# ScalarE and VectorE in source order in an attention loop, GpSimd too at a layer's end, weights split one sum sooner

## The chip, the cores and the metric

The kernel runs on one core of a Trainium2 chip. The metric is the device time of one execution in microseconds. The engines are named as in the profile: PE (TensorE, matmuls), PEld (its weight loads), ACT (ScalarE), DVE (VectorE), POOL (GpSimd) and SP (SyncE, which issues the DMAs here).

## The reference

Two layers, each an attention and a spectral filter on x of 2048 rows by 1024 columns, in float32:

```python
def attn(x, wqkv, wo):                 # 32 heads of 32 columns
    q, k, v = split_heads(x @ wqkv)
    p = softmax(q @ k.T * 32 ** -0.5)
    return merge_heads(p @ v) @ wo
def spec(x, w_r, w_i):
    return irfft2(rfft2(x) * (w_r + 1j * w_i))
for _ in range(2):
    x = x + attn(layernorm(x), wqkv, wo)
    x = x + spec(layernorm(x), w_r, w_i)
```

## The kernel before

**The attention's tiles.** The 32 heads are worked on in 8 groups of four, g = 0 to 7. For one group the 2048 queries are taken in 4 chunks c of 512, and the keys in 16 tiles kt of 128. One (g, c, kt) is called a unit here. A unit has three parts. `S` makes the scores with 12 matmuls (L540) into two PSUM tiles `s`, and ACT takes the exp of each (L544, 128x1024) into a tile `p`. `PV` multiplies them with V (16 matmuls, L550). `add` sums the two `p` tiles into two accumulators on DVE (L561 for the first pair of units of a chunk, L563 for the others). The pool of `p` tiles has eight buffers, four units' worth.

**A chunk's end.** `fin` sums the accumulators over the keys with 8 matmuls (L569, called z in this document), and DVE turns, inverts and turns back the sums and scales the chunk's output with them (L570 to L576). `out` splits it into two f16 halves `ohl`: ACT casts the high one (L582), POOL subtracts for the low one (L583).

**Filler.** All products but PV use f16 high and low halves. While group g runs through its 64 units, PE also makes the q, k and v sums of later groups, a few matmuls behind every second unit: `qk_chunk` (24 matmuls a sum, L327) and `v_tiles` (L371). A q or k sum ends in `split`: ACT writes the high half from PSUM (L166) and DVE the low one (L167); POOL squares it (L331) for a bound on the scores (L344, L346). A v sum needs ACT alone. There is one PSUM bank for these sums (`psX`), so the next sum's first matmul waits until its split is done.

**Weights.** `Weights.prep` is a generator for the weights of one phase (the k, q or v sums of one group). It asks for its first three pieces by DMA (L247), then with each step splits one piece (L166, L167; in layer 0 also a maximum, L256 and L257). A q or k weight has two pieces, a v weight four (`wv`). `filler` steps the preparation of the next phase once after each sum.

**The last two groups.** In g=6 `load_wo` splits the projection's weights, and `wo_parts` starts the output projection over the groups that are done (L429, 42 matmuls a tile of 128 rows, drained by DVE at L449). In g=7 `wo_rest` adds the last group's share to 12 of the 16 row tiles: 6 matmuls, then DVE adds (L458), takes statistics (L460, L481), and the tile is written out.

**A layer's end.** The last four row tiles need the last chunk. `first` does their matmuls over the other groups, `last` the rest, with statistics. Every tile is layer-normed for the spectral stage, which wants it folded: `fold` adds and subtracts two halves on POOL (L145, L146), and the fold is scaled on DVE (L160, L161). The scale is a power -0.5 on POOL (L120) and one Newton step on DVE (L121 to L124). `fold_rests` does the 12 earlier tiles with one power for all. The spectral stage starts with transposes on PE (L742), whose every first operand takes rows from all 16 tiles.

**What sets the order.** The loop stands in a manual schedule for PE alone: PE does its instructions in the order of the source. On ACT, DVE, POOL and SP a scheduler places them at build time. In the source, `add` follows `S` by two units: in the step of unit u the scores of u come first, then PV and the adds of u-2, then a piece of filler.

Of the kernel before, what the change touches and what calls it, by code (L numbers as in the profile page):

```python
# [6 lines left out]
F32 = mybir.dt.float32  # L7
# [5 lines left out]
ALU = mybir.AluOpType  # L13
# [99 lines left out]
    return st  # L113


def ln_scale(nc, sm, cst, mv, n=1):

    v, r, q = (sm.tile([128, n], F32, name=f"{c}{n}") for c in "vrn")
    nc.vector.tensor_scalar(v, mv[:, 1::2], 1e-5, None, op0=ALU.add)
    nc.gpsimd.tensor_tensor(r, v, cst["mhalf"].broadcast_to([128, n]), op=ALU.pow)  # L120
    nc.vector.tensor_mul(q, r, r)  # L121
    nc.vector.tensor_mul(q, q, v)
    nc.vector.tensor_scalar(q, q, -0.5, 1.5, op0=ALU.mult, op1=ALU.add)
    nc.vector.tensor_mul(r, r, q)  # L124
    return r


def ln_stats(nc, sm, cst, st, mv):

    nc.vector.bn_aggr(mv, st)  # L130
    return ln_scale(nc, sm, cst, mv)


def layernorm(nc, sm, cst, x, out):
# [6 lines left out]
def fold(nc, x, out, a):  # L141

    xv = x.rearrange("p (a u g q) -> p g a u q", a=8, g=2, q=8)[:, :, a]
    ov = out.rearrange("p (u g a q) -> p g a u q", g=2, a=8, q=8)[:, :, a]
    nc.gpsimd.tensor_tensor(ov[:, 0], xv[:, 0], xv[:, 1], op=ALU.add)  # L145
    nc.gpsimd.tensor_tensor(ov[:, 1], xv[:, 0], xv[:, 1], op=ALU.subtract)  # L146


def fold_norm(nc, sm, cst, st, out):

    mv = sm.tile([128, 2], F32, name="mv")
    r = ln_stats(nc, sm, cst, st, mv)
    b = sm.tile([128, 1], F32, name="b")
    nc.vector.tensor_scalar(b, mv[:, 0:1], 2.0, None, op0=ALU.mult)
    norm_folded(nc, out, out, b, r)


def norm_folded(nc, x, out, b, r):
    xv, ov = (a.rearrange("p (u g q) -> p g u q", g=2, q=64) for a in (x, out))
    nc.vector.tensor_scalar(ov[:, 0], xv[:, 0], b, r, op0=ALU.subtract, op1=ALU.mult)  # L160
    nc.vector.tensor_scalar(ov[:, 1], xv[:, 1], r, None, op0=ALU.mult)  # L161
# [8 lines left out]
def run(g):  # L170
    for _ in g:
        pass
# [93 lines left out]
def attention(nc, tc, layer, ap, xin, yd, wts, wo, cst, dram, flags):  # L266
# [6 lines left out]
    sq, on, on2, sm = ap.sq, ap.on, ap.on2, ap.sm  # L273
# [109 lines left out]
    def sums(ph):  # L383
        return 8 if ph[0] == "v" else 4

    def filler():
        run(prep(phases[0]))
        for i, ph in enumerate(phases):
            nxt = prep(phases[i + 1]) if i + 1 < len(phases) else iter(())
            for n in range(sums(ph)):  # L390
                yield from (v_tiles if ph[0] == "v" else qk_chunk)(ph, n)
                next(nxt, None)
            run(nxt)


# [27 lines left out]
    def wo_mm(p, c, t, n, ds, start=True, stop=True):  # L423

        for d in ds:
            oh, ol = ((olast[c][:, i] if d == 7 else osb[c][:, i, d])[:, t * 128:t * 128 + 128] for i in range(2))
            wh, wl = (wo_t[i][d // 4][:, d % 4, n * 512:n * 512 + 512] for i in range(2))
            for i, (a, b) in enumerate(((oh, wh), (oh, wl), (ol, wh))):
                nc.tensor.matmul(p, a, b, start=start and d == ds[0] and i == 0, stop=stop and d == ds[-1] and i == 2)  # L429
                yield  # L430
# [21 lines left out]
    def wo_last(c, t, p, src, y, start):  # L452

        for n in range(2):
            run(wo_mm(p[:, n], c, t, n, (7,), start=start))
        st = sm.tile([128, 2, 6], F32, name="st")
        r0 = c * 512 + t * 128
        nc.vector.scalar_tensor_tensor(y, p.rearrange("p n c -> p (n c)"), 1.0 / (SO * SW), src, op0=ALU.mult, op1=ALU.add)  # L458
        for n in range(2):
            nc.vector.bn_stats(st[:, n], y[:, n * 512:n * 512 + 512])  # L460
        nc.sync.dma_start(yd[r0:r0 + 128, :], y)
        return st
# [14 lines left out]
    mvs = sm.tile([128, 24], F32, name="mvs")  # L477
# [4 lines left out]

    def fold_rests():

        r = ln_scale(nc, sm, cst, mvs, 12)
        b = sm.tile([128, 12], F32, name="b12")
        nc.vector.tensor_scalar(b, mvs[:, 0::2], 2.0, None, op0=ALU.mult)
        for t in SPILL + [t for t in range(12) if t not in SPILL]:
            o = ap.x[:, t]
            f = o if t in SPILL else pp.tile([128, 1024], F32, name="xn", tag="p")  # L490
            fold(nc, wo_dst[t], f, slice(0, 8))
            norm_folded(nc, f, o, b[:, t:t + 1], r[:, t:t + 1])


# [16 lines left out]
    for c in range(NCH):  # L511
        t = 4 * c + 4
# [44 lines left out]
    def add(g, c, kt):  # L557
        for hf in range(2):
            p = P[g, c, kt, hf]
            if kt == 1:  # L560
                nc.vector.scalar_tensor_tensor(acc[hf], P[g, c, 0, hf], 1e-34, p, op0=ALU.add, op1=ALU.add)  # L561
            elif kt:
                nc.vector.tensor_add(acc[hf], acc[hf], p)  # L563
# [25 lines left out]
    pend, done, late = [], [], []  # L589
# [3 lines left out]
    def slots(f, sums, n, steps):  # L593

        while sums:
            k = max(1, int(n / sums + 0.5))
            m = -(-steps // k)
            for i in range(0, steps, m):
                while left_norms:
                    norms()  # L600
                for _ in range(min(m, steps - i)):
                    next(f, None)
                n -= 1
                yield sums - (i + m >= steps)
            sums -= 1

    with tc.manual_schedule(engines={mybir.EngineType.PE}):
        for g in range(NG):
            todo = sum(sums(ph) for ph in beside.get(g, []))
            sl = slots(fill, todo, 22 if g == NG - 2 else 32, 24)  # L610
            wsl = slots(wof, 4, 10, 21)
            for u in range(NCH * NKT):
                c, kt = divmod(u, NKT)
                S(g, c, kt)
                if kt % 2 == 0:
                    for w in pend:
                        PV(*w)
                    late = pend
                    pend = []
                for w in late[:1]:  # L620
                    add(*w)
                    if w[2] == NKT - 1:
                        fin(*w[:2])
                        done = [w[:2]]
                late = late[1:]
                if kt == 5 and done:
                    out(*done.pop())
                pend.append((g, c, kt))
                if kt % 2 == 0:
                    continue  # L630
                if todo:
                    todo = next(sl)
                elif g == NG - 2:
                    if left:
                        run(lwo)
                        left = 0
                    if next(wsl, None) is not None and u == NCH * NKT - 1:
                        run(wsl)
                elif g == NG - 1:
                    t = rests[0] if rests else 16  # L640
                    if (t // 4 < c - 1 or t // 4 == c - 1 and kt >= 7) and (kt % 4 == 3 or not parts):
                        wo_rest(rests.pop(0))
                    elif parts:
                        parts -= 1
                        for _ in range(21):
                            next(wof)
                if g == NG - 2 and todo < 4:
                    for _ in range(2):
                        if left > (8 if todo == 3 else 0):
                            next(lwo, None)  # L650
                            left -= 1
        for w in pend:
            PV(*w)
        for w in late + pend:
            add(*w)
        run(wof)
        for t in rests:
            wo_rest(t)
        ps, xs = [], []

        def first(t, ds):
            if ds[0] == 0:
                ps.append(psS.tile([128, 2, 512], F32, name="s"))
                xs.append(xres(3, t))
            for n in range(2):
                run(wo_mm(ps[t][:, n], 3, t, n, ds, start=ds[0] == 0, stop=False))

        def last(t):
            o = ap.x[:, 12 + t]
            st = wo_last(3, t, ps[t], xs[t], xs[t], False)  # L670
            fold(nc, xs[t], o, slice(0, 8))
            fold_norm(nc, sm, cst, st, o)
        first(0, range(7))
        fin(NG - 1, NCH - 1)
        out(NG - 1, NCH - 1, nc.vector)
        fold_rests()
        first(1, range(7))
        last(0)
        first(2, range(7))
        last(1)  # L680
        first(3, range(4))
        last(2)
        first(3, range(4, 7))
        last(3)
    psum.close()
    small.close()

# [491 lines left out]
```

## Time and profile before

| | us |
|---|---|
| median of 3 runs | 4025.53 (4022.86 to 4028.82) |
| the profiled execution's own time | 4029.87 |
| its span in the trace | 4028.0 |
| ACT's exps, L544, 2048 of them | 2163.9 busy |
| DVE's adds, L563, 1792 of them | 2163.1 busy |
| POOL | 634.9 busy |
| z of the last chunk, layer 0 and 1 | at 1696.31 and 3690.98 |
| first spectral transposes (L742), layer 0 and 1 | at 1758.13 and 3759.27 |

The span is one execution, taken by the profiler; sums of the prediction are made against its own time. A profile line names a source line, an engine, an operation and its tiles (out<-in); a wait stands in brackets as the idle time ahead of an instruction and who ended it. Idle time counts only on the engine that bounds a stage.

### The profile page before, as it was taken

What the parts mean: (1) busy time and instruction counts of PE and PEld (TensorE: products, weight loads), DVE (VectorE), ACT (ScalarE), POOL (GpSimd) and SP (SyncE); (2) the same over time, 40 slices, a digit from 0 to 9 for tenths busy, and PEclk for the clock granted to TensorE, in tenths of its full rate; (3) what the DMA queues carried; (4) which work ended last, traced back from release to release, by engine and by line L of the source; (5) the groups of instructions that cost most, each with busy time, mean ns of one, the idle gap of its engine ahead of it and who ended that gap; (6) DMA issues with size and microseconds to landing.
All of it is one profiled execution on the core that took longest, in us unless ns stands there. A gap on an engine that the chain in (4) does not pass through costs nothing. (4 is left out here: it accounts for less than half of the span.)

```text
span 4028.0 us, 80149 instructions
## 1 busy us (share of the span) xinstructions
PE 3791.8 (94%) x33204; PEld 1680.2 (42%) x33204; DVE 3257.1 (81%) x3897; ACT 2863.0 (71%) x3533; POOL 634.9 (16%) x585
## 2 busy tenths in 40 slices
PE   7999999999999999979989999999999999997898
PEld 5322423342234233368854234233422432332787
DVE  6789888888988977766766898888889889788456
ACT  4677777787778866448746787788878888663485
POOL 1111011101110100314321110111011101003143
PEclk9999999999999999989989999999999999999999
DMA  3000000000000211143120000000000002121333
GB/s 114 19 22 17 7 22 14 14 9 22 17 12 7 87 51 66 53 152 125 57 84 14 27 17 7 22 17 14 7 22 17 12 9 87 53 72 49 141 101 100
DMA packets 97561, 177.32 MB, mean 44 GB/s; under 512 B 7201, under 2 KB 52897, under 8 KB 96161
## 3 DMA queue, kind: packets, MB, share of 16 engines
q1 hardware_dynamic: 97040, 172.03, 12.7%
q8 instruction: 262, 4.29, 0.5%
q14 instruction: 115, 0.93, 0.1%
q10 hardware_dynamic: 144, 0.07, 0.0%
HBM read 123.83 MB, written 48.23 MB: 43 GB/s over the span
## 5 line engine op out<-in xcount | busy, mean ns | idle before, releaser
L544 ACT ACTIVATE p<-s,bias 128x1024 f32<-128x1024 f32 x2048 | 2163.9, 1111 | 534.6 <-PE s L540 527.9
L563 DVE TENSOR_TENSOR R<-R,p 128x1024 f32<-128x1024 f32 x1792 | 2163.1, 1259 | 163.2 <-ACT p L544 160.7
L550 PE MATMUL o<-p,R 128*32 128x512 f32 x8192 | 996.0, 604 | 0.0
L327 PE MATMUL x<-big,wqk 128*128 128x512 f16 x2880 | 678.6, 380 | 18.0 <-DVE R L167 9.3
L540 PEld LDWEIGHTS <-R 32*128 32x128 f16 x12288 | 239.1, 92 | 845.6 <-issue 728.6
L540 PE MATMUL s<-R 32*128 32x512 f16 x6144 | 444.4, 380 | 49.2 <-ACT p L544 44.4
L540 PE MATMUL s<-Q,R 32*128 32x512 f16 x6144 | 442.2, 378 | 27.8 <-ACT p L544 16.7
L327 PEld LDWEIGHTS <-wqk 128*128 128x128 f16 x3072 | 276.8, 98 | 449.1 <-issue 162.8
L550 PEld LDWEIGHTS o<-p,R 128*32 128x32 f32 x8192 | 214.8, 109 | 529.7 <-issue 529.1
L371 PEld LDWEIGHTS <-big 128*128 128x128 f16 x3072 | 291.9, 98 | 102.3 <-issue 56.3
L371 PE MATMUL x<-wv,big 128*128 128x256 f16 x2688 | 321.1, 275 | 5.9 <-DVE big L167 2.9
L561 DVE SCALAR_TENSOR_TENSOR R<-p 128x1024 f32<-128x1024 f32 x128 | 153.9, 1204 | 195.6 <-ACT p L544 195.6
L331 POOL TENSOR_TENSOR sq<-R 128x512 bf16<-128x512 f16 x96 | 149.3, 1555 | 970.8 <-ACT R L166 970.6
L583 POOL TENSOR_TENSOR ohl<-zt,ohl 128x512 f16<-128x512 f32 x62 | 83.2, 1342 | 1178.4 <-ACT ohl L582 1178.4
L429 PE MATMUL x<-big 128*128 128x512 f16 x1008 | 228.0, 380 | 0.0
L429 PEld LDWEIGHTS <-big 128*128 128x128 f16 x1344 | 126.8, 98 | 177.6 <-issue 35.4
L582 ACT CAST ohl<-zt 128x512 f16<-128x512 f32 x64 | 39.6, 618 | 140.0 <-DVE zt L576 98.6
L861 DVE TENSOR_TENSOR H<-G,H 128x512 f16<-128x512 f32 (+1 forms) x68 | 46.7, 687 | 104.1 <-ACT H L860 104.0
L331 POOL TENSOR_TENSOR sq<-Q 128x512 bf16<-128x512 f16 x32 | 48.9, 1529 | 444.6 <-ACT Q L166 444.6
L813 PE MATMUL ps<-cbi,H 128*128 128x256 f16 (+1 forms) x792 | 99.1, 273 | 5.6 <-ACT H L860 3.7
L806 ACT COPY U<-ps 64x256 f32<-64x256 f32 (+1 forms) x272 | 97.0, 357 | 7.8 <-PE ps L813 2.6
L806 ACT COPY B<-ps 64x256 f32<-64x256 f32 (+1 forms) x272 | 97.0, 356 | 6.7 <-PE ps L813 2.4
(417 smaller groups left out, 3256.3 us busy)
## 6 DMA issues: line engine op xcount, KB each, us to landing
wst<-in_wp SPq DMA_DIRECT2D x96, 256.0 KB, 2.8
R<-y SPq DMA_DIRECT2D x32, 512.0 KB, 5.2
w<-in_w SPq DMA_DIRECT2D x60, 256.0 KB, 2.7
od<-ohl SPq DMA_DIRECT2D x56, 256.0 KB, 2.4
big<-od SPq DMA_DIRECT2D x16, 896.0 KB, 6.4
y<-R SPq DMA_DIRECT2D x20, 512.0 KB, 2.6
R<-in_x SPq DMA_DIRECT2D x16, 512.0 KB, 6.8
wst<-in_wo SPq DMA_DIRECT2D x32, 256.0 KB, 3.1
```

The source lines that it names most:

```text
L327: nc.tensor.matmul(ps, a, b, start=d == 0 and i == 0, stop=d == 7 and i == 2)
L331: nc.gpsimd.tensor_tensor(nrm[ph][:, c], t[:, 0], t[:, 0], op=ALU.mult)
L371: nc.tensor.matmul(ps[:, j], l, r, start=d == 0 and i == 0, stop=d == 7 and i == 2)
L429: nc.tensor.matmul(p, a, b, start=start and d == ds[0] and i == 0, stop=stop and d == ds[-1] and i == 2)
L540: nc.tensor.matmul(s[h // 2][:, h % 2], K[g][r, a, kt * 128:kt * 128 + 128], Q[g][r, b, c * 512:c * 512 + 512], start=i == 0, stop=i == 2)
L544: nc.scalar.activation(p, s[hf], AF.Exp, bias=bias[g], scale=SCALE / (SQ * SQ))
L550: nc.tensor.matmul(O[g, c][32 * h:32 * h + 32], V[g][:, kt, 32 * h:32 * h + 32], P[g, c, kt, h // 2][:, h % 2], start=kt == 0, stop=kt == ...
L561: nc.vector.scalar_tensor_tensor(acc[hf], P[g, c, 0, hf], 1e-34, p, op0=ALU.add, op1=ALU.add)
L563: nc.vector.tensor_add(acc[hf], acc[hf], p)
L583: eng.tensor_tensor(t[:, 1], r, t[:, 0], op=ALU.subtract)
L806: nc.scalar.copy(ov[64 * r:64 * r + 64, a0:a0 + m, x], tl[64 * x:64 * x + 64, :m, r])
L813: nc.tensor.matmul(out, l, r, start=k == 0, stop=k == len(mm_) - 1)
```

## The change

1. In the loop ACT and DVE are put under manual order as well: they too do their instructions in the order of the source.
2. After the loop's last projections a second manual schedule begins, for PE, ACT, DVE and POOL.
3. `ln_scale` is parted into `ln_root` (variance, power on POOL) and `ln_newton`. `fold_rests` becomes a generator, stepped fold by fold between the last tiles. `last` does statistics, power and fold of a last tile, a new `scale` its Newton step and norm.
4. At the end of the loop the adds that are left (`late`) come before the last PV, and each PV is followed by its own add.
5. `filler` steps the preparation of the next weights twice after each sum but a phase's first.

```diff
-def ln_scale(nc, sm, cst, mv, n=1):
+def ln_root(nc, sm, cst, mv, n=1):
-    v, r, q = (sm.tile([128, n], F32, name=f"{c}{n}") for c in "vrn")
+    v, r = (sm.tile([128, n], F32, name=f"{c}{n}") for c in "vr")
     nc.vector.tensor_scalar(v, mv[:, 1::2], 1e-5, None, op0=ALU.add)
     nc.gpsimd.tensor_tensor(r, v, cst["mhalf"].broadcast_to([128, n]), op=ALU.pow)
+    return v, r
+def ln_newton(nc, sm, v, r, n=1):
+    q = sm.tile([128, n], F32, name=f"n{n}")
     nc.vector.tensor_mul(q, r, r)
...
                 yield from (v_tiles if ph[0] == "v" else qk_chunk)(ph, n)
-                next(nxt, None)
+                for _ in range(1 + (n > 0)):
+                    next(nxt, None)
...
             fold(nc, wo_dst[t], f, slice(0, 8))
+            yield
             norm_folded(nc, f, o, b[:, t:t + 1], r[:, t:t + 1])
...
-    with tc.manual_schedule(engines={mybir.EngineType.PE}):
+    E = mybir.EngineType
+    with tc.manual_schedule(engines={E.PE, E.Activation, E.DVE}):
...
+        for w in late:
+            add(*w)
         for w in pend:
             PV(*w)
-        for w in late + pend:
             add(*w)
         run(wof)
         for t in rests:
             wo_rest(t)
-        ps, xs = [], []
+    with tc.manual_schedule(engines={E.PE, E.Activation, E.DVE, E.Pool}):
+        ps, xs, sc, folds = [], [], {}, fold_rests()
...
         def last(t):
-            o = ap.x[:, 12 + t]
-            st = wo_last(3, t, ps[t], xs[t], xs[t], False)
-            fold(nc, xs[t], o, slice(0, 8))
-            fold_norm(nc, sm, cst, st, o)
+            st = wo_last(3, t, ps[t], xs[t], xs[t], False)
+            mv = sm.tile([128, 2], F32, name="mv")
+            nc.vector.bn_aggr(mv, st)
+            b = sm.tile([128, 1], F32, name="b")
+            nc.vector.tensor_scalar(b, mv[:, 0:1], 2.0, None, op0=ALU.mult)
+            sc[t] = (b, *ln_root(nc, sm, cst, mv))
+            fold(nc, xs[t], ap.x[:, 12 + t], slice(0, 8))
+
+        def scale(t):
+            b, v, r = sc[t]
+            o = ap.x[:, 12 + t]
+            norm_folded(nc, o, o, b, ln_newton(nc, sm, v, r))
+
+        def some(n):
+            for _ in range(n):
+                next(folds, None)
         first(0, range(7))
         fin(NG - 1, NCH - 1)
         out(NG - 1, NCH - 1, nc.vector)
-        fold_rests()
+        some(8)
         first(1, range(7))
         last(0)
+        some(2)
+        scale(0)
         first(2, range(7))
+        some(2)
         last(1)
+        run(folds)
+        scale(1)
         first(3, range(4))
         last(2)
         first(3, range(4, 7))
+        scale(2)
         last(3)
+        scale(3)
```

PE's order stays as it was but for a few rows. Up to the loop the line numbers of the changed kernel are higher by 5 to 7: its L172 is L167 of before, L568 is L561, L570 is L563, L577 to L583 are L570 to L576, L150 and L151 are L145 and L146, L126 to L129 are L121 to L124.

DVE before, in the last chunk of g=0 in layer 1: adds (into R, from p), the low halves of three k sums (R<-x,R) and of a weight (wqk), and then the next chunk's first add with `fin`'s first step (zt).

```order
L563 TENSOR_TENSOR R<-R,p 128x1024 x8
L167 SCALAR_TENSOR_TENSOR R<-x,R 128x512
L563 TENSOR_TENSOR R<-R,p 128x1024 x12
L167 SCALAR_TENSOR_TENSOR R<-x,R 128x512
L563 TENSOR_TENSOR R<-R,p 128x1024 x8
L167 SCALAR_TENSOR_TENSOR R<-x,R 128x512
L167 SCALAR_TENSOR_TENSOR wqk<-wst,wqk 128x512 x2
L561 SCALAR_TENSOR_TENSOR R<-p 128x1024
L570 STREAM_TRANSPOSE zt<-s 128x512
```

DVE after, in the same chunk, from its first two units' adds to `fin`'s first step.

```order
L568 SCALAR_TENSOR_TENSOR R<-p 128x1024 x2
L570 TENSOR_TENSOR R<-R,p 128x1024 x4
L172 SCALAR_TENSOR_TENSOR R<-x,R 128x512
L570 TENSOR_TENSOR R<-R,p 128x1024 x4
L172 SCALAR_TENSOR_TENSOR wqk<-wst,wqk 128x512 x2
L570 TENSOR_TENSOR R<-R,p 128x1024 x8
L172 SCALAR_TENSOR_TENSOR R<-x,R 128x512
L570 TENSOR_TENSOR R<-R,p 128x1024 x8
L172 SCALAR_TENSOR_TENSOR R<-x,R 128x512
L570 TENSOR_TENSOR R<-R,p 128x1024 x4
L577 STREAM_TRANSPOSE zt<-s 128x512
```

Each low half of a sum stands four adds sooner: the first behind the adds of units 1 to 3 (it stood behind unit 5), the last ahead of the chunk's last four adds (it stood behind them). `fin` no longer has adds of the next chunk between its steps.

POOL before, at the end of layer 0: the last `ohl` of the loop, folds (R or xn) of the 12 earlier tiles, and the power for all twelve (r, from v).

```order
L583 TENSOR_TENSOR ohl<-zt,ohl 128x512 x5
L145 TENSOR_TENSOR R<-R 128x8x8x8
L146 TENSOR_TENSOR R<-R 128x8x8x8
L145 TENSOR_TENSOR R<-wv 128x8x8x8 x2
L146 TENSOR_TENSOR R<-wv 128x8x8x8 x2
L145 TENSOR_TENSOR xn<-R 128x8x8x8
L146 TENSOR_TENSOR xn<-R 128x8x8x8
...
L145 TENSOR_TENSOR xn<-R 128x8x8x8
L120 TENSOR_TENSOR r_18270<-v_18269,mhalf 128x12
L146 TENSOR_TENSOR xn<-R 128x8x8x8
L145 TENSOR_TENSOR xn<-R 128x8x8x8
```

POOL after, at the same place; the power with `128x1` belongs to last tile 0, whose folds read xres.

```order
L590 TENSOR_TENSOR ohl<-zt,ohl 128x512 x5
L120 TENSOR_TENSOR r_18273<-v_18272,mhalf 128x12
L150 TENSOR_TENSOR R<-R 128x8x8x8
L151 TENSOR_TENSOR R<-R 128x8x8x8
L150 TENSOR_TENSOR R<-R 128x8x8x8
L151 TENSOR_TENSOR R<-R 128x8x8x8
...
L150 TENSOR_TENSOR xn<-R 128x8x8x8
L151 TENSOR_TENSOR xn<-R 128x8x8x8
L120 TENSOR_TENSOR r_18378<-v_18377,mhalf 128x1
L150 TENSOR_TENSOR R<-xres 128x8x8x8
L151 TENSOR_TENSOR R<-xres 128x8x8x8
L150 TENSOR_TENSOR xn<-R 128x8x8x8
```

The power for twelve tiles was behind most of the folds and now is ahead of them all; the folds of the last four earlier tiles moved behind last tile 0.

DVE before, at the end of layer 0, from the last `wo_rest` on.

```order
L458 SCALAR_TENSOR_TENSOR R<-s,R 128x1024
L563 TENSOR_TENSOR R<-R,p 128x1024
L460 BN_STATS st<-R 128x6 x2
L481 BN_AGGR mvs<-st 128x2
L119 TENSOR_SCALAR v_18269<-mvs 128x12
L487 TENSOR_SCALAR b_18278<-mvs 128x12
L121 TENSOR_TENSOR n_18271<-r_18270 128x12
L122 TENSOR_TENSOR n_18271<-n_18271,v_18269 128x12
L123 TENSOR_SCALAR n_18271<-n_18271 128x12
L124 TENSOR_TENSOR r_18270<-r_18270,n_18271 128x12
L160 TENSOR_SCALAR R<-R,b_18278,r_18270 128x8x64
L161 TENSOR_SCALAR R<-R,r_18270 128x8x64
```

DVE after, from the loop's last adds on.

```order
L570 TENSOR_TENSOR R<-R,p 128x1024 x4
L577 STREAM_TRANSPOSE zt<-s 128x512
L579 RECIPROCAL rc<-zt 128x16
L580 TENSOR_TENSOR fr<-fr,rc 128x16
L582 STREAM_TRANSPOSE zt<-rc 128x512
L583 SCALAR_TENSOR_TENSOR zt<-oc,zt 128x512
L590 TENSOR_TENSOR ohl<-zt,ohl 128x512
L119 TENSOR_SCALAR v_18272<-mvs 128x12
L126 TENSOR_TENSOR n_18276<-r_18273 128x12
L127 TENSOR_TENSOR n_18276<-n_18276,v_18272 128x12
L128 TENSOR_SCALAR n_18276<-n_18276 128x12
L129 TENSOR_TENSOR r_18273<-r_18273,n_18276 128x12
```

Before, the power's Newton step and the norms came right behind the statistics (`fin` begins 16 rows behind the first norm); after, `fin` and `out` (ohl, L590) come first, and the variance that the power waits for stands behind them.

More of the change, by code (lines that the diff above doesn't have):

```diff
@@ L130, in ln_stats @@
     nc.vector.bn_aggr(mv, st)
-    return ln_scale(nc, sm, cst, mv)
+    return ln_newton(nc, sm, *ln_root(nc, sm, cst, mv))
 def layernorm(nc, sm, cst, x, out):
@@ L483, in fold_rests @@
     def fold_rests():
-        r = ln_scale(nc, sm, cst, mvs, 12)
+        r = ln_newton(nc, sm, *ln_root(nc, sm, cst, mvs, 12), 12)
         b = sm.tile([128, 12], F32, name="b12")
```

## Prediction

> **What bounds the kernel now.** I read the page first, then PE's waits, then chunks of the loop by windows, then the timeline.
>
> ```profile
> span 4028.0 us, 80149 instructions
> PE 3791.8 (94%) x33204; PEld 1680.2 (42%) x33204; DVE 3257.1 (81%) x3897; ACT 2863.0 (71%) x3533; POOL 634.9 (16%) x585
> L544 ACT ACTIVATE p<-s,bias 128x1024 f32<-128x1024 f32 x2048 | 2163.9, 1111 | 534.6 <-PE s L540 527.9
> L563 DVE TENSOR_TENSOR R<-R,p 128x1024 f32<-128x1024 f32 x1792 | 2163.1, 1259 | 163.2 <-ACT p L544 160.7
> ```
>
> PE is busy for 94% of the span, so a time is gained or lost where PE waits. Who makes it wait (total us, times, longest):
>
> ```profile
> PE s L540 <- ACT p L544: 61.1, 59, 4.7
> PE s L429 <- ACT ohl L582: 40.3, 2, 20.2
> PE ps L742 <- DVE R L160: 18.6, 2, 12.0
> PE x L327 <- DVE R L167: 9.3, 12, 0.9
> PE x L327 <- DVE Q L167: 6.5, 6, 1.5
> ```
>
> The loop over 64 chunks fills most of the span. Windows from one row-sum matmul (z, L569) to the next, with PE's, PEld's, DVE's, ACT's and POOL's busy time and the granted clock:
>
> ```profile
> 750.10:801.20 51.10, 47.43 (x444) 17.24 (x443) 42.71 (x44) 37.20 (x41) 8.57 (x7) 0.93 0.05 17
> 937.70:993.70 56.00, 47.73 (x408) 14.09 (x407) 49.17 (x57) 39.26 (x44) 6.28 (x4) 0.94 0.11 34
> 1132.70:1178.70 46.00, 44.96 (x440) 16.96 (x436) 41.06 (x40) 37.21 (x41) 9.06 (x7) 1.00 0.06 18
> 2293.40:2339.90 46.50, 46.31 (x415) 14.31 (x411) 42.50 (x41) 37.74 (x41) 9.05 (x8) 1.00 0.03 8
> 2566.50:2619.10 52.60, 47.25 (x407) 13.87 (x404) 44.49 (x45) 39.24 (x44) 7.23 (x4) 0.97 0.11 36
> ```
>
> A clean chunk (2293.40) has PE idle for 0.2 us and DVE idle for 4.0: PE bounds it, DVE is next by 4 us of 46. Two of the others carry the preparation of the v weights:
>
> ```profile
> 960.23 20.54 SPq L247 DMA_DIRECT2D wst<-in_wp  x6
> 965.53 0.63 ACT L166 ACTIVATE wv<-wst 128x512 f16<-128x512 f32 x1 [5.28 <-DMA wst<-in_wp]
> 967.22 1.86 PE L540 MATMUL s<-R 32*128 32x512 f16 x12 [4.68 <-ACT p L544]
> 969.00 3.26 PE L550 MATMUL o<-p,R 128*32 128x512 f32 x16
> ```
>
> ACT stood at a weight split for its DMA, the exps behind it came late, PE waited 4.68 us, and then ran for some 5 us at half speed (L540 x12 takes 0.83 elsewhere).
>
> **1. Weights in source order.** ACT now splits the wv parts two at a time, each pair one filler sum after its load was asked for, so the DMA has landed. A disturbed chunk falls from 52.6 to about 46 in layer 1 and from 56.0 to 46.5 in layer 0; three of each: −20 and −29. In layer 0 the windows from 750.10 and its like in g=1 are 5.1 and 3.2 above the clean 46.0 (1132.70): −8. PE's waits for psX (L327 on L167, 9.3 + 6.5) shrink, since the low half no longer waits behind four adds: −12 of 15.8. Together **−69**; bounds −50 (a wait of this kind comes back once per group) and −75.
>
> **2. DVE in source order, in the loop.** Before, the low half of a filler sum (L167) stands behind every add whose exps are done. Now it stands two units (four adds) earlier, and DVE may not pass it: it idles until the sum's last matmul and ACT's high half are through, with four adds left behind it. What this costs is read at a chunk's end, where z needs the last add. Chunk 3 of g=0, layer 1:
>
> ```profile
> 2326.25 4.87 DVE L563 TENSOR_TENSOR R<-R,p 128x1024 f32<-128x1024 f32 x4
> ...
> 2333.39 2.76 PE L327 MATMUL x<-big,wqk 128*128 128x512 f16 x12
> ...
> 2336.19 0.60 ACT L166 ACTIVATE R<-x 128x512 f16<-128x512 f32 x1 [0.57 <-PE x L327]
> ...
> 2336.92 0.68 DVE L167 SCALAR_TENSOR_TENSOR R<-x,R 128x512 f16<-128x512 f32 x1
> ...
> 2339.89 1.06 PE L569 MATMUL s<-R,ones 128*32 128x512 f32 x8 [0.18 <-ACT p L544]
> ```
>
> The last add had ended before the low half at 2336.92, three us ahead of z. Now: high half until 2336.79, low half until 2337.5, then the adds of the last two units, four that took 4.87 in the row above (POOL squares beside them): 2342.3. z goes from 2339.89 to 2342.3, **+2.4**, and nothing gives it back, since PE has no idle time in the next chunk to make it up in. Where the last low half stands further ahead of z, DVE gains about 0.3 us per unit (two adds take 2.3, a unit on PE 2.6), but waits there once more and has a mqk reduction on its way; walking such chunks row by row I get +1.9 to +3.5. Four chunk ends of each pair of groups carry it (three in the even g, one where the odd g's q sums run; v sums have no low half), over 6 pairs. At 2.7 each: **+65**; bounds +46 and +84. In layer 0 the weights' low halves and maxima (L167, L256, 0.7 each) now stand in that queue as well, 1.5 for each of six weights: **+9**.
>
> **3. The last two groups.** The same order holds for the output projection: L449 in g=6, and L458, L460, L481 in g=7, now ahead of the last two units' adds.
>
> ```profile
> 1574.87 1.47 PE L429 MATMUL s<-big,ohl 128*128 128x512 f16 x6
> ...
> 1577.26 1.22 DVE L458 SCALAR_TENSOR_TENSOR R<-s,R 128x1024 f32<-128x1024 f32 x1
> ...
> 1579.53 1.28 DVE L460 BATCH_NORM_STATS2 st<-R 128x6 f32<-128x512 f32 x2
> ...
> 1580.51 1.07 PE L569 MATMUL s<-R,ones 128*32 128x512 f32 x8
> 1580.61 2.12 ACT L544 ACTIVATE p<-s,bias 128x1024 f32<-128x1024 f32 x2
> 1580.84 0.21 DVE L481 BATCH_NORM_AGGREGATE mvs<-st 128x2 f32<-128x12 f32 x1
> ```
>
> The matmuls end at 1576.34; 1.22 + 1.28 + 0.21 and four adds (4.6) later it is 1583.7, against z at 1580.51: +3.2, at two chunk ends of a layer. With L449 (0.68) alone it is 1.7 at two more: +20 for both layers. Group 6's own sums and wo splits are put at +5, the first chunk of a layer at +4: **+33** in all; bounds 0 (the slack that DVE has here: 10 us a chunk) and +40.
>
> **4. The clock.** Some 24 of the new waits reach 2.4 us or more. In this trace a wait of 3.15 halved PE's speed and one of 3.52 did not:
>
> ```profile
> 201.40 1.86 PE L540 MATMUL s<-R 32*128 32x512 f16 x12 [3.15 <-ACT p L544]
> 203.19 3.64 PE L550 MATMUL o<-p,R 128*32 128x512 f32 x16
> ...
> 2966.73 1.15 PE L540 MATMUL s<-R 32*128 32x512 f16 x12 [3.52 <-ACT p L544]
> ```
>
> Such a halving costs 1.0 + 1.7 us (1.86 for 0.83, 3.64 for 1.92). I let one in four of the 24 meet it: **+16**; bounds 0 and +50. The Trainium skill ("TensorE: Matmul & The Clock Gate", section "HAM oscillation — how this bites in real kernels") asks only that PE's idle gaps stay under about 3.4 us. By it this term would be 0 and the sum 16 less; the 3.15 above speaks against it as a sharp limit, so I keep the term.
>
> **5. The layer's end.** Here PE's 20 us for ohl go: `fin` and `out` now come ahead of the norms on DVE. What is late next is POOL.
>
> ```profile
> 1663.91 1.26 POOL L145 TENSOR_TENSOR R<-R 128x512 f32<-128x512 f32 x1 [19.87 <-PE o L550]
> ...
> 1707.67 2.31 POOL L120 TENSOR_TENSOR r<-v,mhalf 128x12 f32<-128x12 f32 x1
> 1709.96 1.25 POOL L146 TENSOR_TENSOR xn<-R 128x512 f32<-128x512 f32 x1
> ...
> 1714.90 1.43 DVE L160 TENSOR_SCALAR R<-R,b,r 128x512 f32<-128x512 f32 x1
> 1716.25 0.47 DVE L161 TENSOR_SCALAR R<-R,r 128x512 f32<-128x512 f32 x1
> 1716.64 0.53 DVE L160 TENSOR_SCALAR R<-R,b,r 128x512 f32<-128x512 f32 x1
> ...
> 1726.72 2.74 PE L429 MATMUL s<-big,ohl 128*128 128x512 f16 x6 [20.18 <-ACT ohl L582]
> ...
> 1758.13 1.98 PE L742 MATMUL ps<-ident,R 128*128 128x128 f32 x8 [6.57 <-DVE R L160]
> ```
>
> Before, folds ran from 1663.9 on, inside the loop. Now the pow for twelve tiles is first on POOL, behind `fin`, ACT's cast and `out` on DVE (about 1701.5), so it ends at 1703.8 and eight tiles are folded at 1723.3 (16 folds, 1.22 apart). Only then has last tile 0 its DVE steps (3.0) and its pow and fold (3.0); folds of four tiles follow to 1739, last tile 1 to 1742.6, and tiles 2 and 3, one after the other at 6 to 7 us, end with their norms at 1756.5. The transposes at L742 need all of that: 1.6 us earlier than 1758.13. That is the lower bound. The upper one adds twelve norms of 0.93 between the folds, if neither runs beside the other: 1767.6. The row at 1714.90 (1.43 beside a fold, 0.53 without) shows that they do block each other. The middle, 1762, is +4 in layer 0; in layer 1, where L742 came 6 us later after z, it is −3. Both ends: **+1**; bounds −10 and +12. The Trainium skill ("SBUF — State Buffer", section "Who interferes with whom") says that whichever of the two issues first holds the port for its whole instruction; by that the upper bound holds at both ends, and the sum is 11 more.
>
> **Sum.** −69 + 65 + 9 + 33 + 16 + 1 = +55 on the profiled run's own 4029.87 (span 4028.0): 4085. That run stands 4.3 above the median of the runs shown, 4025.53; against those I say **4080**.
>
> **Rivals.**
> *DVE keeps ahead (faster).* The place is z. If the low half's wait leaves at most two adds behind it, not four, z comes within the 3.7 us that PE spends on S, PV, S behind the last filler matmul (2336.15 to 2339.89), and terms 2 to 4 fall to nothing. For it: eight buffers of exps let ACT and PE run on meanwhile, and the clean window has 4 us of idle DVE. Against it: those 4 us are at a chunk's start, where the stall isn't. Then only term 1 and some of the ohl wait count: 4025.5 − 69 + 0 to −20, about 3950. Chance 0.24.
> *Even.* The new waits take back just what term 1 gave, because the adds catch up in the chunks without a late low half: terms 2 and 3 at half, 4 at 0. 4025.5 − 69 + 54 + 1 = 4011 to 4040. Chance 0.18, half of it within 0.2%.
> *The clock falls at most chunk ends.* Terms 2 and 4 at their upper bounds: 4080 + 19 + 34 = 4133, and with the folds blocked 4144. Chance 0.13.
> *The change doesn't do what it says*: the order of both programs shows that it does; no chance.
> My forecast keeps 0.45, with its own range 4045 to 4115.
>
> **How the numbers follow.** 0.2% is 8 us, about what a measurement here can tell from no change. Faster: 0.24 + 0.04 of the even case = 0.28; within 0.2%: 0.09; slower: 0.45 + 0.13 + 0.05 = 0.63. The range leaves out the half of the first rival below 3950 and what lies above 4145: 3950 to 4145.
>
> **What would show it.** Term 1: no window of the loop at 52 or more in g=0 to 5, and no long ACT wait for wst. Term 2: PE waits for DVE's add at z, 1 to 3 us each, some 20 to 30 times, and DVE idle at L167. Term 3: the same behind L458. Term 4: clock below 1.00 right behind those waits. Term 5: no 20 us wait for ohl, POOL busy without a break from 1702 on, and L742 waiting for DVE's norm behind POOL's fold. I am wrong if z has no wait, or if the folds run freely beside the norms.

## The result, and the profile after

The changed kernel takes 4126.51 us (median of 4 runs, 4124.43 to 4127.43) against 4024.22 for the kernel before: a ratio of 1.0251, 95% interval 1.0234 to 1.0269. It is 2.5% slower. The forecast was slower, 4080 in a range of 3950 to 4145; 46 us of the loss were not in it.

The page of the changed kernel, its first lines and three groups (busy, mean ns, idle time before and its main releaser):

```profile
span 4124.8 us, 79748 instructions
PE 3832.6 (93%) x33204; PEld 1679.5 (41%) x33204; DVE 3277.5 (79%) x3897; ACT 2859.2 (69%) x3533; POOL 646.2 (16%) x585
L551 ACT ACTIVATE p<-s,bias 128x1024 f32<-128x1024 f32 x2048 | 2168.1, 1111 | 654.4 <-PE s L547 449.9
L570 DVE TENSOR_TENSOR R<-R,p 128x1024 f32<-128x1024 f32 x1792 | 2119.1, 1246 | 35.4 <-ACT p L551 35.3
L576 PE MATMUL s<-R,ones 128*32 128x512 f32 x512 | 123.3, 683 | 71.1 <-DVE R L570 65.7
```

Each engine does as many instructions as before; PE is busy for 41 us longer. What is new is the last line: z (L576, L569 before) now waits 71 us, nearly all of it for DVE's add. PE's waits, and two of DVE's, say more:

```profile
PE s L576 <- DVE R L570: 65.7, 34, 3.5
PE ps L771 <- DVE R L165: 51.3, 2, 25.9
PE s L547 <- DVE mqk L351: 38.0, 22, 3.8
PE s L435 <- DVE xres L464: 25.5, 2, 15.8
DVE R L172 <- ACT R L171: 162.9, 54, 5.8
DVE wqk L172 <- ACT wqk L171: 74.8, 14, 19.6
```

PE used to wait for exps (61.1, the longest of them behind weights) and for ohl (40.3); both are out of the list's head. In their place PE waits for DVE: at z, at the mqk reduction (14.1 before) and at the layer's end (L771 was L742, 18.6 before). And DVE itself stands at low halves whose high halves ACT hasn't written: adds used to fill that time. Windows from z to z in the changed kernel, for four of the chunks shown of before (columns as there):

```profile
951.80:1000.30 48.50, 46.78 (x400) 13.56 (x400) 40.19 (x40) 34.61 (x36) 5.81 (x4) 0.96 0.02 7
1147.60:1199.50 51.90, 47.76 (x438) 17.30 (x438) 44.48 (x45) 35.07 (x38) 10.59 (x7) 0.94 0.05 17
2348.50:2397.00 48.50, 46.62 (x414) 14.34 (x411) 41.43 (x42) 39.90 (x43) 6.69 (x8) 1.00 0.05 18
2628.10:2676.50 48.40, 46.66 (x402) 13.61 (x404) 40.25 (x40) 34.97 (x37) 5.81 (x4) 0.96 0.02 7
```

The two chunks that carried the v weights fell from 56.0 and 52.6 to 48.5 and 48.4, not to 46. The clean one (46.5) rose to 48.5, and the one at 1147.6, which was clean at 46.0, takes 51.9: the v weights are split there now, and PE waits there 2.91 us for the mqk reduction.

The whole span in parts, from the times of z, of each layer's first scores and first transposes in the traces. "First" is from the first scores to the first z, "end" from the last z to the transposes; layer 0 / layer 1:

| | first | groups 0-5 | group 6 | group 7 | end |
|---|---|---|---|---|---|
| before | 44.5 / 44.5 | 1141.8 / 1115.0 | 207.3 / 207.0 | 173.8 / 173.8 | 61.8 / 68.3 |
| after | 52.3 / 51.2 | 1157.1 / 1125.4 | 218.3 / 218.2 | 183.2 / 183.2 | 71.6 / 77.5 |
| change | +14.5 | +25.7 | +22.2 | +18.8 | +19.0 |

The sum, 100.2, less 3.4 in the rest, is the 96.8 by which the span grew.

### The profile page after: what moved, and what is told of

Its sections match the earlier page's. It is cut to its first block, busy times and chain, and to the rows that moved or that the text cites. A ratio compares the mean times of both kernels' runs of the same rounds, so it can differ in the third digit from the quotient of the medians.

```text
span 4124.8 us, 79748 instructions
## 1 busy us (share of the span) xinstructions
PE 3832.6 (93%) x33204; PEld 1679.5 (41%) x33204; DVE 3277.5 (79%) x3897; ACT 2859.2 (69%) x3533; POOL 646.2 (16%) x585
## 5 line engine op out<-in xcount | busy, mean ns | idle before, releaser
L570 DVE TENSOR_TENSOR R<-R,p 128x1024 f32<-128x1024 f32 x1792 | 2119.1, 1246 | 35.4 <-ACT p L551 35.3
L332 PE MATMUL x<-big,wqk 128*128 128x512 f16 x2880 | 687.2, 384 | 12.9 <-ACT wqk L171 5.4
L332 PEld LDWEIGHTS <-wqk 128*128 128x128 f16 x3072 | 277.2, 98 | 465.8 <-issue 176.9
L547 PE MATMUL s<-R 32*128 32x512 f16 x6144 | 434.2, 379 | 25.5 <-DVE mqk L351 23.3
L590 POOL TENSOR_TENSOR ohl<-zt,ohl 128x512 f16<-128x512 f32 x62 | 100.7, 1625 | 1515.6 <-ACT ohl L589 1515.6
L336 POOL TENSOR_TENSOR sq<-R 128x512 bf16<-128x512 f16 x96 | 121.2, 1262 | 806.7 <-ACT R L171 806.7
L576 PE MATMUL s<-R,ones 128*32 128x512 f32 x512 | 123.3, 683 | 71.1 <-DVE R L570 65.7
L172 DVE SCALAR_TENSOR_TENSOR R<-x,R 128x512 f16<-128x512 f32 x88 | 60.4, 686 | 136.2 <-ACT R L171 136.2
L568 DVE SCALAR_TENSOR_TENSOR R<-p 128x1024 f32<-128x1024 f32 x128 | 158.2, 1276 | 0.0
L577 DVE STREAM_TRANSPOSE zt<-s 128x512 f32<-128x512 f32 x64 | 45.9, 717 | 123.8 <-PE s L576 123.8
L96 ACT COPY tt<-ps 128x512 f32<-128x512 f32 x64 | 37.5, 586 | 146.2 <-PE ps L771 143.0
L171 ACT ACTIVATE R<-x 128x512 f16<-128x512 f32 x88 | 52.6, 598 | 111.6 <-PE x L332 111.5
```

The lines of the kernel that those rows point to most:

```text
L332: nc.tensor.matmul(ps, a, b, start=d == 0 and i == 0, stop=d == 7 and i == 2)
L336: nc.gpsimd.tensor_tensor(nrm[ph][:, c], t[:, 0], t[:, 0], op=ALU.mult)
L547: nc.tensor.matmul(s[h // 2][:, h % 2], K[g][r, a, kt * 128:kt * 128 + 128], Q[g][r, b, c * 512:c * 512 + 512], start=i == 0, stop=i == 2)
L576: nc.tensor.matmul(z[32 * h:32 * h + 32], cst["ones"], acc[h // 2][:, h % 2], start=True, stop=True)
L590: eng.tensor_tensor(t[:, 1], r, t[:, 0], op=ALU.subtract)
```

## The experiments

Theory A is that VectorE's fixed order costs, since it stands at instructions whose input isn't there with adds behind them, and at the layer's end GpSimd's. The rivals are ScalarE's order (B), and those named with each run. All ratios are to the kernel before.

**1. Which engine's order costs, and the end: e1, e2, e3, e4.** Four kernels, each the changed one with one thing put back; e1 has the end's source of before as well.

```diff
 e1: -    with tc.manual_schedule(engines={E.PE, E.Activation, E.DVE, E.Pool}):
     +    with tc.manual_schedule(engines={E.PE}):
 e2: -    with tc.manual_schedule(engines={E.PE, E.Activation, E.DVE}):
     +    with tc.manual_schedule(engines={E.PE, E.Activation}):
 e3: +    with tc.manual_schedule(engines={E.PE, E.DVE}):
 e4: -                for _ in range(1 + (n > 0)):
     -                    next(nxt, None)
     +                next(nxt, None)
```

> The changed loop with the layer end of before (its source order, PE alone in manual order there). In the changed kernel the stretch from the last z to the first spectral transposes is 71.6 and 77.5 us, before it was 61.8 and 68.3. Theory A (GpSimd's late power and the folds and norms blocking each other make the new end longer): both stretches go back to 62 to 69 us, the time falls by 16 to 20, to about 4108. Rival (the end is late because the loop hands over its last adds late): the stretches stay at 70 us and more, the time at 4120 to 4127.

Measured: 4121.26, ratio 1.0241 (1.0224 to 1.0258). The two stretches fell to 59.8 and 67.6, 21.7 in all, as theory A had it; but group 7 rose from 183.2 to 190.6 and 192.2, and 16 of the 22 were given back there. With the old end the folds run in group 7 again, where an add takes up to 2.3 us beside a fold instead of 1.2, and in the fixed order it holds up all that DVE has behind it: at the end of group 7 in layer 0 four adds took 8.60, and z waited 5.58 for them. The theory's stretch was right, its time was not.

> The changed kernel, but in the loop VectorE is placed by the scheduler again; PE and ScalarE keep source order. Theory A (VectorE's order is what costs in the loop: it stands at the low halves, drains and mqk reductions with adds behind them): PE's waits for DVE at z (65.7 us) and for mqk (38.0 us) nearly go, the loops of both layers fall by 80 to 110 us, the time to 4020 to 4050. Rival B (ScalarE's order costs: high halves ahead of exps): the loops keep most of their excess, 4100 or more.

Measured: 4000.69, ratio 0.9935 (0.9919 to 0.9952), below even what theory A gave, and 0.65% faster than before. Groups 0 to 5 take 1107.1 and 1084.2, group 7 173.6 and 173.7. The wait for DVE at z is gone from the list; what leads in the loop is this:

```profile
PE s L547 <- ACT p L551: 27.2, 27, 6.8
PE x L332 <- DVE R L172: 8.0, 8, 2.1
```

So DVE's fixed order alone costs 126 us, and the rest of the change wins 24. That is the main result.

> The changed kernel, but in the loop ScalarE is placed by the scheduler again; PE and VectorE keep source order. Theory A: nothing is won, 4115 to 4150 (the high halves come no sooner, and weight splits may stand at their DMA again as before, some 5 us each). Rival B: the time falls to 4020 to 4060.

Measured: 4278.9, ratio 1.0623 (1.0605 to 1.064): rival B falls, but the loss is far over what A gave. The waits of ACT and of SP's queue show why:

```profile
ACT wv L171 <- DMA wst<-in_wp: 83.7, 24, 5.0
ACT wqk L171 <- DMA wst<-in_wp: 54.7, 23, 5.0
SPq L252 <- DVE wm L261: 357.6, 25, 74.8
SPq L252 <- DVE wqk L172: 260.8, 29, 76.0
```

A load of weights waits for the buffer that DVE, in source order, reads late; ACT, which the scheduler has splitting early, stands at that load with the exps behind it (PE waited 153.2 us for exps). What is new here is ACT's stand, 138.4 us against 6.6 in the changed kernel; SP's waits for DVE are longer in the changed kernel (596.4 and 451.7), where nothing stands at the loads. That a split placed early by the scheduler and a buffer read late in the fixed order are what don't go together is read from these rows; no run separates them.

> The changed kernel with one step of weight preparation after each sum, as before. Theory A: the step count hardly matters, 4126 plus or minus 8, the weight splits only move within their chunks. Rival (two splits in a row on ScalarE and VectorE make the queue ahead of the adds longer and cost 1 us each): 4095 to 4115. A second rival (the weights of the next phase come too late without the second step): 4140 or more.

Measured: 4120.18, ratio 1.0234 (1.0217 to 1.0251). With DVE's order in force the second step gains nothing, as theory A had it.

**2. The low halves: e5, e9, e12.** VectorE keeps its source order here; the source itself is changed. In e5 the loop gives a sum's low half behind the next odd unit's adds, in e9 behind the next unit's; e12 adds to e9 that the weights' low halves come behind the next odd unit's adds. In e9 and e12 `low_halves()` stands without the `if kt % 2`; `both` is empty in the loop, so its sums go by the `else`.

```diff
 qk_chunk:
-        split(nc, t[:, 0], t[:, 1], ps, SQ / (SX * SW))
+        if both:
+            split(nc, t[:, 0], t[:, 1], ps, SQ / (SX * SW))
+        else:
+            nc.scalar.activation(t[:, 0], ps, AF.Copy, scale=SQ / (SX * SW))
+            lows.append((t[:, 1], ps, t[:, 0]))
...
 loop, behind the adds:
                 late = late[1:]
+                if kt % 2:
+                    low_halves()
...
 e12, Weights.prep:
-            split(nc, h, l, st[i], SW)
+            if self.later is None:
+                split(nc, h, l, st[i], SW)
+            else:
+                nc.scalar.activation(h, st[i], AF.Copy, scale=SW)
+                self.later.append((l, st[i], h))
...
 e12, loop, behind the adds:
+                if kt % 2:
+                    while wts.later:
+                        lo, w, hi = wts.later.pop(0)
+                        nc.vector.scalar_tensor_tensor(lo, w, SW, hi, op0=ALU.mult, op1=ALU.subtract)
```

> The changed kernel, VectorE still in source order, but in the loop the source gives a q or k sum's low half two units (four adds) later than its high half, right behind the next odd unit's adds; weights, drains and mqk reductions stay where they are. Theory A (VectorE stands at a low half whose high half is not there yet, with four adds behind it): groups 0 to 5 fall by 50 to 80 of the 91 us that the scheduler's placing won there, PE's waits for DVE at z (65.7 us) fall below 25; the time is 4045 to 4080. Rival C (any fixed order on VectorE costs, because waits for exps, maxima and weights come at other times each chunk): at most 20 us are won, 4105 or more.

Measured: 4211.71, ratio 1.0468 (1.0451 to 1.0486). A clear miss: 85 us slower than the changed kernel. z waits less (43.2, 20 times), but PE waits for psX and DVE for weights:

```profile
PE x L332 <- DVE R L350: 58.6, 32, 4.3
PE x L332 <- DVE Q L350: 52.7, 18, 5.7
PE x L385 <- DVE R L350: 18.5, 4, 5.3
DVE wqk L172 <- ACT wqk L171: 133.2, 28, 19.6
```

There is one PSUM bank for the sums (L332 and L385 are L327 and L371 of before; L350 is the low half). Two units later is too late for the next sum, which wants the bank; and DVE stands longer at the weights' low halves, which stayed ahead.

> As e5, but the low half comes one unit (two adds) later than its high half, not two. After e5 the theory is: in a fixed order a low half has a deadline on both sides. Too early and VectorE idles in front of it with four adds behind (PE waits at z), too late and the one psX bank is not free for the next sum's first matmul (PE waited 130 us for it in e5). One unit later the bank is free in time (the next sum starts after the second unit) and only two adds are left over: PE's waits for psX stay below 30 us, those at z fall from 65.7 to below 30, groups 0 to 5 fall below the changed kernel's 1157 and 1125 by 20 to 40 each; 4050 to 4090. Rival (a low half anywhere in a fixed order costs the same, because DVE has no slack at all): 4115 or more.

Measured: 4098.68, ratio 1.0184 (1.0167 to 1.0201), 28 better than the changed kernel but short of the expectation; groups 0 to 5 take 1148.6 and 1107.0.

```profile
PE s L585 <- DVE R L579: 44.0, 21, 3.3
PE x L332 <- DVE Q L350: 30.2, 10, 3.8
DVE wqk L172 <- ACT wqk L171: 99.8, 28, 19.6
```

The wait at z (L585 here) was still 44 us and those for psX 53, where below 30 was expected for each, and DVE's longest stand was not at a sum's low half but at a weight's.

> e9 with the weights' low halves given later in the source too, behind the next odd unit's adds. In e9 VectorE still stood 99.8 us in front of low halves of wqk, and PE waited 44 us for it at z and 53 us for psX. Theory: these stands were put ahead of the adds by the fixed order just as the sums' low halves were; with them gone VectorE's waits for ACT at low halves of wqk fall by 50 us or more and the time to 4060 to 4080. Rival (those stands lie in parts where VectorE has time, before the loops and at their first chunks): 4090 to 4100.

Measured: 4015.72, ratio 0.9983 (0.9973 to 0.9992), 83 better than e9 and 111 better than the changed kernel, past what was expected. z in e12 (L591), and windows from z to z for chunks 1, 2 and 3 of groups of even number:

```profile
PE s L591 <- DVE R L585: 15.2, 10, 2.5
2545.00:2589.60 44.60, 44.60 (x406) 13.21 (x402) 40.76 (x40) 36.28 (x38) 8.08 (x4) 1.00 0.02 7
2230.00:2275.50 45.50, 45.50 (x412) 13.90 (x408) 42.19 (x41) 37.34 (x40) 10.85 (x5) 1.00 0.06 19
2275.50:2321.60 46.10, 46.10 (x412) 14.18 (x408) 41.30 (x41) 38.05 (x41) 6.74 (x8) 1.00 0.05 18
```

PE is busy for the whole of each window. Groups 0 to 5 take 1093.5 and 1078.3: 20 us less than with the scheduler's placing in e2. So a fixed order on DVE isn't dear in itself there; the places of the low halves in it are. Groups 6 and 7, whose drains and statistics e12 leaves in their places, take 33 more than in e2, and as a whole e12 is 15 slower than e2. What the weights' low halves would do alone, with the sums' left where they were, wasn't tried, so the two shares aren't known apart.

**3. What the second step is worth: e8, e11.** e8 is the kernel before with ScalarE added to its manual order; e11 is e6 (below) with one step.

> The kernel before with one thing changed: ScalarE too keeps source order in the loop and at the layer's end. Theory A (term 1 alone, the weight splits no longer stand at their DMA; in e2 groups 0 to 5 were 34.7 and 30.8 us shorter than before): groups 0 to 5 1105 to 1112 and 1083 to 1090 us, first chunks 5 us longer as in e2; 3970 to 3985. Rival (the win needs the second step of weight preparation as well): 3995 or more.

Measured: 4012.82, ratio 0.9973 (0.9963 to 0.9984); groups 0 to 5 1118.1 and 1102.5. The rival held: the rest of the win needs the second step.

> e6 (VectorE free in the loop, old end) with one step of weight preparation after each sum. Theory: with ScalarE in source order and one step the v weights' last part is late for their first sum, which is what e8 showed (PE waited 25.5 us for wv there): groups 0 to 5 at 1115 to 1120 and 1100 to 1105 us, 4005 to 4015. Rival (e8 differs from e6 for another reason): 3980 to 3990.

Measured: 4011.58, ratio 0.9974 (0.9961 to 0.9986); groups 0 to 5 1117.6 and 1101.5, as in e8, with the wait that was named:

```profile
PE x L376 <- DVE wv L172: 25.5, 7, 4.6
```

With one step the v weights end too late for their first sum. The second step is worth 29 us (e6 against e11) where DVE is free, and nothing where it isn't (e4).

**4. The end and the first chunk: e6, e7, e10.** All three have VectorE free in the loop, as e2. e6 has the old end; e7 the new end without GpSimd in its manual order; e10 is e7 with the first weights prepared ahead of the loop.

```diff
 e7:  -    with tc.manual_schedule(engines={E.PE, E.Activation, E.DVE, E.Pool}):
      +    with tc.manual_schedule(engines={E.PE, E.Activation, E.DVE}):
 e10:      both.clear()
      +    run(prep(phases[0]))
...
           def filler():
      -        run(prep(phases[0]))
```

> VectorE free in the loop as in e2, and the layer end of before as in e1. Theory A: the ends win 20 as in e1 (62 and 68 us from z to the transposes) and the folds in the last group of the loop cost nothing, since VectorE can do other adds while one waits: 3978 to 3985. Rival: the folds inside the last group slow its adds as in e1 (group 7 went from 183.2 to 190.6 and 192.2): 3990 to 4001.

Measured: 3982.31, ratio 0.9901 (0.9884 to 0.9917); the ends take 62.5 and 69.3, group 7 173.7 and 173.6. The folds in the loop cost nothing once DVE may do another add meanwhile.

> VectorE free in the loop as in e2, and the new layer end with GpSimd placed by the scheduler; PE, ScalarE and VectorE keep the new order there. Theory A (what makes the new end long is GpSimd's late start behind the power): folds run early, from z to the transposes it is 48 to 58 us instead of 71.6 and 77.6, the time 3960 to 3980. Rival (the end is held by the chain of the last tiles through power, Newton step and norm): 64 to 72 us, 3988 to 4000.

Measured: 3975.29, ratio 0.9879 (0.9862 to 0.9895). The ends take 54.0 and 66.5, 17.6 and 11.1 less than in e2: GpSimd's fixed order is what made the new end long. Layer 0 and the time came out by theory A, but layer 1's 66.5 lies where the rival had it. There DVE, still in fixed order, stands at a reduction of flags that POOL now does behind its folds, with the last ohl behind it, and PE waits 14.4 us for that ohl. PE's wait at the transposes in e7, 51.2 in e2, and DVE's stand:

```profile
PE ps L771 <- DVE R L165: 22.3, 2, 11.7
3663.15 0.17 DVE L1118 TENSOR_SCALAR fa<-fa 128x2 f32<-128x2 f32 x1 [18.23 <-POOL fa L1117]
```

> e7 with one more change: the first weights of the loop's filler are prepared ahead of the loop, outside of the manual order. With ScalarE in source order the stretch from the first scores to the first z was 49.4 to 49.7 us against 44.5 before; there PE waits 2.7 us for wqk and goes on at half speed. Theory: both stretches go back to 44 to 46 us, the time falls by 8 to 10, to 3964 to 3969. Rival (something else in the chunk is late): 3973 to 3978.

Measured: 3964.88, ratio 0.9855 (0.9839 to 0.9872), the fastest kernel of this study, 1.5% below the one before. Both first stretches are back at 44.5. e12's loop with this end and these first weights wasn't run.

## Why the prediction was right, and where it was short

The direction and the main mechanism were right: z waits for DVE's add, and DVE for low halves. The time, 4126.5, lies in the stated range but above the forecast's own 4045 to 4115. It is near the 4133 of the rival whose clock falls at most chunk ends, but that is chance: z is slow at 17 of 64. Two of the four parts agree, two were too small.

**Weights in source order (−69).** Right in size: groups 0 to 5 lost 65.5 in e2 against before (34.7 and 30.8). The six disturbed chunks alone fell by 53 there (49 was said). The part for psX (−12) is not in it: those waits are 14.9 in e2 against 15.8, and fall to 6.2 only with DVE's order. The forecast gave one figure for ScalarE's order and the splitting in pairs; 30 of it (1117.6 and 1101.5 in e11 against 1104.2 and 1084.4 in e6) is the second step.

**DVE in source order (+65, +9), and the clock (+16).** The mechanism held: from e2 to the changed kernel groups 0 to 5 rise by 91.2, against 90. That the sum agrees so well is partly luck. PE waits for an add at z 24 times there, as often as was counted, but 47 us in all, 2.0 each and not 2.7. The mqk waits, for which no term stood, rise from 3.3 to 28.2 there, and PE's busy time by 39: a z that waits is longer, and some are slow. In the whole span z waits for the last add 34 times. The chunk that was worked out, in the changed kernel's timeline (start, duration, engine, line; idle time in brackets):

```profile
2391.78 0.60 ACT L171 ACTIVATE R<-x 128x512 f16<-128x512 f32 x1 [0.53 <-PE x L332]
2392.41 0.69 DVE L172 SCALAR_TENSOR_TENSOR R<-x,R 128x512 f16<-128x512 f32 x1 [1.45 <-ACT R L171]
2393.01 4.96 DVE L570 TENSOR_TENSOR R<-R,p 128x1024 f32<-128x1024 f32 x4
...
2396.99 1.67 PE L576 MATMUL s<-R,ones 128*32 128x512 f32 x6 [1.88 <-DVE R L570]
2398.04 0.39 PE L349 MATMUL s<-sq,bones 128*32 128x512 bf16 x2
2398.48 0.60 PE L576 MATMUL s<-R,ones 128*32 128x512 f32 x2
```

DVE waits 1.45 at the low half, then four adds take 4.96 (4.87 was assumed), and z starts 1.88 late. Its second half needs the very last add (ended at 2397.97), so z takes 2.09 instead of 1.07 and ends some 2.9 late; +2.4 lay between. What failed is the sharing out inside the term: the weights' low halves got +9, the sums' +65. In groups 0 to 5 giving the sums' one unit later wins 27 (e9 against after), and giving the weights' later too wins 84 more (e12 against e9). A wait at a weight is followed by a queue of adds like a wait at a sum, and the working priced it by its own duration alone. These are gains of moving, one upon the other, and not shares of the 91: PE still waits 44.0 at z in e9. The mqk wait (38.0 in the whole span, 14.1 before) is no longer among the long ones in e2 and e12.

**The clock.** It fell, but otherwise than assumed. z's single matmuls, before and after, from the view of one source line (duration ns min/median/max, first and last start):

```profile
L569 PE MATMUL s<-R,ones x512: 592/605/617, 173.4 to 3691.5; 128*32 128x512 f32 x171
L576 PE MATMUL s<-R,ones x512: 588/617/1063, 180.4 to 3780.7; 128*32 128x512 f32 x171
```

In the trace z has matmuls of over 0.9 at 17 chunk ends, and is then about 2.96 long instead of 2.09. Behind 14 of them the first matmuls are slow too (0.61 to 0.64 instead of 0.38), but the scores are at full speed again. So each costs some 1 to 1.5 us by that, not 2.7, and all of them some 17 to 25, an estimate; 16 was said. That agrees, but from more cases at a smaller price. The limit that the Trainium skill gives ("TensorE: Matmul & The Clock Gate", section "HAM oscillation — how this bites in real kernels"), idle gaps of about 3.4 us, did not hold here for the single gap: z at 713.10 was slow behind a wait of 1.88.

**The last two groups and first chunks (+33).** Too small: 55.5. Groups 6 and 7 rose by 41.0 (25 was said), of which 8 stay in e2. The waits for an add at z come to 24.9 there; what was left out is 9.8 of mqk waits and 24 of longer busy time on PE. The first chunks rose by 14.5 (8), of which 10 are ACT standing at the first weights (e10).

**The layer's end (+1, bounds −10 to +12).** The step that failed: the two ends rose by 19.0 together, above the upper bound. In layer 0 the time is that of the upper bound, 71.6 from z to the transposes where it gave 71.3, but it came by another road, so the agreement is chance. In the changed kernel:

```profile
1744.43 2.31 POOL L120 TENSOR_TENSOR r<-v,mhalf 128x12 f32<-128x12 f32 x1 [46.59 <-DVE v L119]
...
1754.01 1.44 POOL L150 TENSOR_TENSOR R<-wv 128x512 f32<-128x512 f32 x1
1754.25 1.48 DVE L166 TENSOR_SCALAR R<-R,r 128x512 f32<-128x512 f32 x1
1755.41 1.44 POOL L151 TENSOR_TENSOR R<-wv 128x512 f32<-128x512 f32 x1
...
1768.22 0.47 DVE L166 TENSOR_SCALAR R<-xn,r 128x512 f32<-128x512 f32 x1
...
1770.73 7.53 PE L435 MATMUL s<-big 128*128 128x512 f16 x24 [9.79 <-DVE xres L464]
...
1791.30 0.81 POOL L120 TENSOR_TENSOR r<-v,mhalf 128x1 f32<-128x1 f32 x1 [5.41 <-DVE v L119]
...
1810.60 1.98 PE L771 MATMUL ps<-ident,R 128*128 128x128 f32 x8 [25.87 <-DVE R L165]
...
3791.59 2.31 POOL L120 TENSOR_TENSOR r<-v,mhalf 128x12 f32<-128x12 f32 x1 [6.76 <-issue]
```

POOL starts with the power, as forecast. Then a fold and a norm take turns, 1.40 us apart, where a fold alone takes 1.22 and a norm alone 0.40 to 0.46: norms run at the pace of folds. The row at 1714.90 of before had said so. By the rule of the Trainium skill ("SBUF — State Buffer", section "Who interferes with whom"), that of the two the one that issues second fully blocks, the sum would have been 11 higher. The trace agrees with the rule for the norms, which take 1.47 beside a fold instead of 0.47; the folds lose only 0.18 each, not a norm's whole time.

So it is DVE that falls behind, and not POOL, whose folds the upper bound let wait for norms. The folds of the first eight tiles end 29.0 behind z, 2.0 above the lower bound's 27.0. The last tiles' statistics then stand on DVE behind Newton steps and norms that are held by folds, and POOL, which was to be busy without a break, stands four times for 4.5 to 5.4 (the row at 1791.30). Of the 11.6 by which the end lies above the lower bound 5.0 arise at last tile 1. In layer 1 the end rose by 9.2 too, where −3 was said. The working let layer 1 be as short as layer 0, but its power starts 11.4 behind z instead of 5.4, behind a reduction of flags that POOL has only there (L1117, at 3784.43; the power is the row at 3791.59).

**Rivals.** DVE didn't keep ahead. With VectorE placed by the scheduler, as in e2 and e7, the time is 3975 to 4001; that rival had been given 3950. Of the signs of being wrong neither came: z waits, and folds and norms hold each other up.

## What to carry to other kernels

A fixed order on an engine that is nearly full makes every instruction that waits for another engine a stop for all that stands behind it: price such a stop by the work queued behind it, not by its own duration. A value made in two steps on two engines, as the halves here, has its second step placed late enough that its input is there, and early enough that its buffer is free; here one unit later won 28 us for the sums and two units lost 85. Put engines under a fixed order one at a time: here ScalarE's won some 65 us in groups 0 to 5 together with the sooner weights (42 of the whole time, e6), VectorE's lost 126 as it was written, and GpSimd's lost 29 at the layers' ends.

## What the runs showed of the hardware

PE lowered its speed behind a wait of 1.88 us (z at 713.1, matmuls of 1.06 instead of 0.60), but not behind another of 1.88 (z at 2396.99), nor behind one of 3.52 in the trace of before. The length of the single wait doesn't decide it; what does isn't shown here.

```profile
713.10 2.11 PE L576 MATMUL s<-R,ones 128*32 128x512 f32 x6 [1.88 <-DVE R L570]
...
715.00 1.07 PE L576 MATMUL s<-R,ones 128*32 128x512 f32 x2
...
1781.06 1.21 DVE L126 TENSOR_TENSOR n<-r 128x1 f32<-128x1 f32 x1
...
1783.42 1.25 POOL L150 TENSOR_TENSOR xn<-R 128x512 f32<-128x512 f32 x1
1783.52 0.15 DVE L128 TENSOR_SCALAR n<-n 128x1 f32<-128x1 f32 x1
```

A fold on GpSimd and a norm on DVE, taking turns, need 1.40 us a pair, where alone they are 1.22 and 0.40 to 0.46 apart. Beside folds even DVE's one-column products (L126 and L127 on 128x1) took 1.2 us instead of 0.16. L128, a TENSOR_SCALAR of one column, took 0.15 beside a fold (at 1783.52), but 1.18 with twelve columns (at 1749.25).
